# Decay rows of one half batch moved to a second set of matmuls, and its values loaded before its keys, in a fused attention and gated-FFN kernel

## The chip, the cores and the metric

The kernel runs on one core of one Trainium2 chip. The metric is device time in microseconds (us) of that core, lower is better. TensorE (PE) does the matmuls, its weight loads have a row of their own (PEld), VectorE (DVE) and ScalarE (ACT) do the elementwise work, GpSimd (POOL) and SyncE (SP) issue most of the DMAs. Each engine works through its own list of instructions in order; so does each DMA queue.

## What is computed

Eight batches, eight heads, 576 positions, head size 64. Attention has a causal mask and a decay that comes from forget gates `f`; its output is the input of a feed-forward block with a three-tap convolution as a gate:

```python
scores = q @ k.T / sqrt(64)
cum = cumsum(log(clip(f, 1e-4, 1.0)))
scores = where(causal, -1e9, scores + cum[..., :, None] - cum[..., None, :])
attn = softmax(scores);  x = (attn @ v)            # heads side by side: 8 x 576 x 512
h = relu(x @ w_in)                                 # 512 -> 1024
gate = sigmoid(conv3(h, conv_w))                   # along the sequence
out = (h * gate) @ w_out                           # 1024 -> 512
```

Inputs and output are FP32. The kernel works in BF16 and FP16 with FP32 sums.

## The kernel before

**Unit of loading: the half batch.** `hb` counts 16 half batches of four heads (`HH` = 4); `b = hb // 2` is the batch. `load_qk` (L106) brings q and k of a half batch by two transposing DMAs on SP's queue (L110), straight into matmul layout: 128 rows, of which the odd ones are the upper halves of the FP32 numbers (taken as BF16) and the even ones the lower halves. The tiles `stq`, `stk` form a ring of four (`RING`). `load_v` (L158) brings the values of a half or a whole batch by five DMAs on SP (L163) with 256-byte pieces; there are two such FP32 tiles, `vf`, one per batch in turn, and `cast_v` (L167) turns a half batch into FP16 `va` on DVE.

**The even rows carry the decay.** They hold lower halves that must go. `clamp` (L116) multiplies them by zero on DVE (L119), or a DMA from a zero tile `consts` does it (`fill`, L129, L132, issued by POOL): q is clamped for `hb` below `CLAMPS` = 8 and filled from there on, k is always clamped. The freed rows then take the decay: rows 96 and 98 of `stk` take the cumulated log gates as a high and a low BF16 part, row 126 of `stq` the high part of the query's, and the facing rows take the constants `PAIR` (about 1.002) and `MINUS`. So one matmul with 128 rows gives scores and decay together. `rows_of` (L135) issues these row loads on POOL, for `hb` = 1 from the SBUF tiles `khi_sb`, `klo_sb` (L140 to L142), later from a DRAM copy `kd` (L144, L146). For `hb` = 0 the rows come early, from a short cut (`rows_first`, L122).

**Work by head pair.** `i` = 0 to 31 counts pairs of heads. For each pair PE does the diagonal blocks of both heads (`diag_scores`, L326, mask added by L330), the blocks below the diagonal per head (`off_scores`, L315), once per half batch the last 64 positions (`tail_scores`, L301); all call `scores` (L296, matmul L298). The PSUM pool `sc` has two buffers. ACT takes the exponentials (L338, L324, L310), PE multiplies by the values (`pv`, L340, L356) into one PSUM buffer `O`, DVE divides by the row sums (`norm`, L359, L367 and L369) and so frees `O`.

**Feed-forward.** Per batch PE transposes the result (L393, L401), multiplies by `w_in` (`moe1`, L420, L425), ACT applies ReLU (L438), DVE does the convolution in two steps (L455, L457), ACT the tanh (L467), DVE the gate (L475), PE multiplies by `w_out` (`moe2`, L484, L487), ACT or DVE empties PSUM (`evac`, L503) and a DMA stores. These share two PSUM buffers `mm`; `ht` has four buffers.

**What sets the order.** The start (L188 to L269) is written out by hand. Everything after is a list of tasks with an engine cost, the tasks that must come first, a key (smaller goes first), buffers taken and given, and for loads a lag to landing. `play` (L713) runs through this list as in a small simulation, and the order in which it starts tasks is the order in which each engine gets its instructions. The numbers in it decide order alone; on the chip each instruction waits for what it needs. `CLAMPS`, `HALVES`, `LANDING`, `QUEUED` and `dma_free` are constants of this plan. In the order by hand, SP's queue holds: `f`, q and k of half batch 0 in two parts each, q and k of half batch 1 (`load_qk(1, 0, 4)`, L235), then the values of batch 0 in two halves (L251, L252). Ahead of these stands

```python
nc.vector.memset(vf_t[0][0:1, 0, 0, 0:1], 0.0)   # L250
```

a one-element write that makes the first load of values wait until DVE has come to that line. Similar one-element writes (`hold`, L149) make the loads of `w_in` and `w_out` wait (L631, L594).

Of the kernel before, what the change touches and what calls it, by code (L numbers as in the profile page):

```python
# [18 lines left out]
def kernel(  # L19
# [26 lines left out]
    HH = 4  # L46
# [88 lines left out]
    def rows_of(hb):  # L135

        tq, tk = stq_t[hb % RING], stk_t[hb % RING]
        c = slice(hb * HH, (hb + 1) * HH)
        if hb == 1:
            nc.gpsimd.dma_start(tk[96:97, 0:HS], khi_sb[c, :])  # L140
            nc.gpsimd.dma_start(tk[98:99, 0:HS], klo_sb[c, :])
            nc.gpsimd.dma_start(tq[126:127, 0:HS], khi_sb[c, :])  # L142
# [3 lines left out]
        nc.gpsimd.dma_start(bass.AP(tensor=tk.tensor, offset=int(tk.offset) + 96 * row, ap=[[2 * row, 2], [1, HS]]),  # L146
                            kd[:, c, :].rearrange("j h s -> j (h s)"))

    def hold(w):  # L149
# [391 lines left out]

    def fill_sources():
        z = consts.bitcast(FP32)
        nc.vector.memset(z, 0.0)
        nc.vector.memset(z[0:2, :], PAIR)
        nc.vector.memset(z[32:33, :], MINUS)
# [10 lines left out]

    last = None
    t_fsrc = task({"DVE": 3.1}, [], -9, fill_sources)
    for hb in range(NHB):  # L560
        key = 2 * hb - 5.5
        ring = [x for j in range(2) for x in t_qk[hb - RING, j]] if hb >= RING else []
        b = hb // 2
        even, landed = [], []
        for s in range(2):
            if hb == 1:
                x = task({"ACT": 0.01}, [], -9, lambda: None, lag=(0.3, 3.8)[s])
# [5 lines left out]
            if hb:  # L573
                t = (stq_t, stk_t)[s][hb % RING]
                rows = [(100, 14, 19)] if s else [(96, 15, 0)] + [(0, 48, 33)] * (hb >= CLAMPS)
                even.append(task({"POOL": 0.55 * len(rows)}, [t_fsrc, x], 2 * hb - 3.5,
                                 lambda t=t, rows=rows: [fill(t, *x) for x in rows],
                                 lag=LANDING + 1.0, dma=0.3 if s or hb < CLAMPS else 1.2))
            if hb and (s or hb < CLAMPS):
                even.append(task({"DVE": 0.9}, [x], (2 * hb - 3 if hb > 1 else -5) + 0.2 * s,  # L580
                                 lambda hb=hb, s=s: clamp(hb, s, 0, 4, 96)))
        t_half = None
        if b == 0 and hb < 2:
            t_half = task({"ACT": 0.01}, [], -9, lambda: None, lag=(6.5, 9.3)[hb])
# [11 lines left out]
        if hb:  # L596
            t_rows[hb] = even + [task({"POOL": 1.1 if hb > 1 else 1.6}, landed, 2 * hb - 3.6 if hb > 1 else -9 if hb > 1 else -1.0,
                                      lambda hb=hb: rows_of(hb), lag=LANDING + 1.0)]
        else:
            t_rows[hb] = []  # L600
        for p in range(2):
            t_cast[hb, p] = task({"DVE": 0.75 if p == 0 else 0.42},
                                 [t_half or t_v[b]] + ([t_pv[2 * hb - 5, 1]] if hb >= 3 else []), 2 * hb - 1.1 + 0.5 * p,
                                 lambda hb=hb, p=p: cast_v(hb, p, nc.vector), lag=0.2)

        for p in range(2):
# [9 lines left out]
            exps = {}  # L616
            x = task({"PE": 0.9}, t_rows[hb], i + 0.1, lambda i=i: diag_scores(i), take="sc")
            t_qk[hb, p] = [t_tail, x]
            mask = task({"ACT": 1.02}, [x], i + 0.1, lambda i=i: diag_exp(i), take="pm", give=[("sc", x)])
            for s in range(2):  # L620
                x = task({"PE": 0.46}, t_rows[hb], i + 0.2 + 0.4 * s, lambda i=i, s=s: off_scores(i, s),
                         take="sc")
                t_qk[hb, p].append(x)
                exps[s] = task({"ACT": 1.02}, [x] + ([t_pv[i - 2, s]] if i >= 2 else []), i + 0.2 + 0.4 * s,
                               lambda i=i, s=s: off_exp(i, s), give=[("sc", x)])
            for s in range(2):
# [3 lines left out]
                                  give=[("pm", mask)] if s else [])  # L630
            t_norm[i] = task({"DVE": 1.05}, [t_pv[i, 1]], i - 0.0, lambda i=i: norm(i) if i else [norm(i), hold(w_in_f16)],  # L631
                             take="xn" if i % PPB == 0 else None, give=[("O", t_pv[i, 0])])
            if i == 0:
                t_win = task({"POOL": 1.0}, [t_norm[0]], -0.5, lambda: nc.gpsimd.dma_start(
                    w_in_f16, moe_w_in.rearrange("(cc p) ff -> p cc ff", p=128)), lag=2.0, dma=6.5)
        if hb % 2:
            early, late = [t_norm[i - 3], t_norm[i - 2]], [t_norm[i - 1], t_norm[i]]
# [8 lines left out]

    start = [PPB * (b0 + nb) + 1.0 for b0, nb in GROUPS]
    start += [start[-1] + 4.0, start[-1] + 6.0]
    t_exp, t_late = [], []
    for g, (b0, nb) in enumerate(GROUPS):  # L650
# [39 lines left out]
        for c in chunks:  # L690
# [19 lines left out]

    AHEAD, QUEUED = 3.0, 8.0

    def play():  # L713
        busy = {"PE": 11.5, "ACT": 12.0, "DVE": 12.0, "POOL": 14.0, "SP": 19.0}
        ready = {e: [] for e in busy}
        dma_free, clock = 21.5, 0.0
        heap, order = [], []
# [111 lines left out]
```

## Time and profile before

| | |
|---|---|
| median of 6 runs | 272.46 us (271.78 to 274.11) |
| the profiled execution, own time | 272.23 us |
| its span, first to last instruction | 270.3 us |
| mean granted TensorE clock | 0.970 |
| busy: PE, DVE, ACT, POOL | 242.3, 227.0, 212.1, 60.5 us |
| DMA queue of SP: share of 16 engines' span | 67.7% |

Shares are of the span. The page cuts the span into 40 slices of 6.76 us and gives each engine's busy share in tenths; PEclk is the TensorE clock that was granted; the DMA row is the mean share of 16 DMA engines. A line of a timeline reads: start in us, duration in us, engine, line of the kernel, operation, what is written and read, how many; in brackets the engine's idle time just before and what ended it. Some matmul records are missing from a trace.

### The profile page before, as it was taken

How to read it: one execution, taken by the hardware profiler on the slowest of the kernel's cores; microseconds unless marked ns; L12 is line 12 of the kernel's file. 1: busy time of each engine (PE TensorE's matmuls, PEld its weight loads, DVE VectorE, ACT ScalarE, POOL GpSimd, SP SyncE). 2: the span in 40 equal slices, each digit the busy share in tenths (PEclk: the TensorE clock that was granted, in tenths of full speed). 3: DMA queues.
4: the chain of work that ended last, by engine and by line, in shares of the span. 5: the costliest groups of instructions: out<-in, count | busy, mean ns of one | idle time of the engine just before them, and what ended most of it. 6: DMA issues, size and time to landing. Idle time of an engine off the chain costs nothing.

```text
span 270.3 us, 6621 instructions
## 1 busy us (share of the span) xinstructions
PE 242.3 (90%) x2602; PEld 166.8 (62%) x2602; DVE 227.0 (84%) x401; ACT 212.1 (78%) x347; POOL 60.5 (22%) x124
## 2 busy tenths in 40 slices
PE   2677789776999999999999999999999999989990
PEld 1246557555777777676776677667776767654640
DVE  5864649979699999999989989999899999978751
ACT  5064649868879999989989899989989998577552
POOL 4391302451121240333315040405010100000000
PEclk9968979997999999999999999999999999999997
DMA  7999999999999999999999999999111201022015
GB/s 132 208 205 189 197 200 201 212 235 185 196 188 192 244 225 202 215 245 221 266 204 204 198 271 164 193 216 237 42 39 41 80 0 66 15 116 80 0 47 226
DMA packets 121284, 44.58 MB, mean 165 GB/s; under 512 B 115560, under 2 KB 116596, under 8 KB 121254
## 3 DMA queue, kind: packets, MB, share of 16 engines
q1 hardware_dynamic: 115088, 32.00, 67.7%
q0 software_dynamic: 5840, 12.01, 17.2%
q8 instruction: 20, 0.33, 0.5%
q10 hardware_dynamic: 326, 0.17, 0.3%
q14 instruction: 10, 0.08, 0.1%
HBM read 13.99 MB, written 9.58 MB: 87 GB/s over the span
## 4 chain that ended last, share of the span: by engine, by line
PE 67%; DMA 8%; issue 6%; DVE 6%; ACT 5%; SPq 5%; POOL 0%; ACTq 0%; DVEq 0%; POOLq 0%
PE mm L487 19%; PE mm L425 18%; PE sc L298 11%; PE O L356 9%; PE sc L330 4%; SPq L110 3%; DMA vf<-in_v_dram 3%; DMA stk<-in_k_dram 2%; PE sc L500 2%; DMA stq<-kd 2%; PE mm L393 2%; ACT po L324 1%; SPq L163 1%; DVE u L457 1%; ACT ht L438 1%
## 5 line engine op out<-in xcount | busy, mean ns | idle before, releaser
L425 PE MATMUL mm<-xt,w_in_f 128*128 128x288 f16 x512 | 79.5, 289 | 1.7 <-DVE xt L413 0.4
L298 PE MATMUL sc<-stq,stk 128*128 128x128 bf16 (+3 forms) x576 | 68.3, 245 | 7.3 <-ACT pm L338 4.7
L324 ACT ACTIVATE po<-sc 128x1024 f16<-128x1024 f32 x64 | 64.7, 1028 | 2.3 <-PE sc L298 1.8
L298 PEld LDWEIGHTS <-stk 128*128 128x128 bf16 x576 | 43.1, 100 | 29.6 <-issue 10.7
L438 ACT ACTIVATE ht<-mm 128x288 f16<-128x288 f32 x128 | 52.1, 414 | 11.4 <-PE mm L425 10.3
L487 PE MATMUL mm<-w_out_f,hg 128*128 128x512 f16 x248 | 58.4, 379 | 0.7 <-ACT xt L411 0.6
L425 PEld LDWEIGHTS <-w_in_f 128*128 128x128 f16 x512 | 47.7, 99 | 18.3 <-issue 3.3
L455 DVE SCALAR_TENSOR_TENSOR u<-ht,cwt 128x576 f32<-128x576 f16 x64 | 51.5, 811 | 5.4 <-ACT ht L438 4.7
L457 DVE SCALAR_TENSOR_TENSOR u<-ht,cwt,u 128x576 f32<-128x576 f16 x64 | 51.5, 811 | 0.5
L467 ACT ACTIVATE hg<-u,cwt 128x576 f16<-128x576 f32 x56 | 43.4, 779 | 2.3 <-DVE u L457 2.2
L475 DVE SCALAR_TENSOR_TENSOR hg<-hg,ht 128x576 f16<-128x576 f16 x56 | 41.7, 751 | 3.5 <-ACT hg L467 3.1
L338 ACT ACTIVATE pm<-sc 128x1024 f16<-128x1024 f32 x32 | 32.9, 1028 | 14.3 <-PE sc L298 14.2
L487 PEld LDWEIGHTS <-hg 128*128 128x128 f16 x248 | 23.6, 98 | 24.2 <-issue 0.9
L356 PE MATMUL O<-va,po 128*128 128x65 f16 x640 | 37.4, 196 | 1.1 <-ACT po L324 1.0
L356 PE MATMUL O<-va,pm 128*128 128x65 f16 x256 | 31.7, 196 | 2.9 <-DVE xn L369 1.7
L356 PEld LDWEIGHTS <-po 128*128 128x128 f16 x640 | 31.4, 99 | 2.1 <-ACT po L324 1.5
L132 POOL DMA_DIRECT2D stq<-consts x23 | 13.3, 583 | 75.0 <-DMA stq<-in_q_dram 28.9
L356 PEld LDWEIGHTS <-pm 128*128 128x128 f16 x256 | 24.6, 100 | 5.7 <-DVE xn L369 2.7
L369 DVE TENSOR_TENSOR xn<-O,rc 128x640 f16<-128x640 f32 x32 | 26.4, 824 | 1.1
L330 PE MATMUL sc<-trib,identb 128*128 128x512 bf16 x64 | 24.9, 390 | 2.0 <-ACT po L324 1.9
L511 ACT ACTIVATE ob<-mm 128x512 f32<-128x512 f32 x23 | 13.7, 598 | 11.0 <-PE mm L487 10.7
L522 POOL DMA_DIRECT2D out_dram<-ob x10 | 7.5, 749 | 41.5 <-ACT ht L438 19.7
(112 smaller groups left out, 223.2 us busy)
## 6 DMA issues: line engine op xcount, KB each, us to landing
vf<-in_v_dram SPq DMA_DIRECT2D x64, 128.0 KB, 4.0
out_dram<-ob POOLq DMA_DIRECT2D x10, 512.0 KB, 5.6
out_dram<-ob SPq DMA_DIRECT2D x10, 256.0 KB, 2.1
stq<-consts POOLq DMA_DIRECT2D x8, 216.0 KB, 4.6
vf<-in_v_dram SPq DMA_DIRECT2D x16, 64.0 KB, 5.3
w_in_f<-in_moe_w_in_dram POOLq DMA_DIRECT2D x1, 1024.0 KB, 10.7
w_out_f<-in_moe_w_out_dram POOLq DMA_DIRECT2D x4, 256.0 KB, 6.4
out_dram<-ob SPq DMA_DIRECT2D x2, 512.0 KB, 2.8
```

Source lines behind the costliest of these rows:

```text
L298: nc.tensor.matmul(sc, stk_t[hb % RING][:, k0:k0 + 128], stq_t[hb % RING][:, q0:q0 + w], start=start, stop=stop, skip_group_check=True)
L324: nc.scalar.activation(p_of[i, s][:, 0:1024], sc_of.pop((i, s)), AF.Exp, scale=SCALE)
L330: nc.tensor.matmul(sc[:, 512 * s:512 * (s + 1)], identb, trib, start=True, stop=False, skip_group_check=True)
L338: nc.scalar.activation(p_of[i, 2], sc_of.pop((i, 2)), AF.Exp, scale=SCALE)
L356: nc.tensor.matmul(O[:, s, 65 * Q:65 * (Q + 1)], w, va[:, h, m, :], start=(m == 0), stop=(m == Q))
L425: nc.tensor.matmul(ps[:, 0:w], w_in_f16[:, cc, 128 * ff:128 * (ff + 1)], xt[:, cc, w * t:w * (t + 1)], start=(cc == 0), stop=(cc == NCC - 1))
L438: nc.scalar.activation(ht[:, 0, HT_0 + w * t:HT_0 + w * (t + 1)], ps[:, 0:w], AF.Relu)
L455: nc.vector.scalar_tensor_tensor(u, hl, cwt[:, ff, 0:1], hc, op0=ALU.mult, op1=ALU.add)
L457: nc.vector.scalar_tensor_tensor(u, hr, cwt[:, ff, 1:2], u, op0=ALU.mult, op1=ALU.add)
L467: nc.scalar.activation(hv, u, AF.Tanh, scale=cwt[:, ff, 2:3])
L475: nc.vector.scalar_tensor_tensor(hv, hv, 1.0, hc, op0=ALU.add, op1=ALU.mult)
L487: nc.tensor.matmul(ps, chunk(g, ff, c), w_out_f16[:, ff, :], start=(ff == 0), stop=(ff == NFF - 1))
```

## The change

Half batch 1 no longer takes its decay in the even rows. Two new tiles, `dk` and `dq`, hold it: rows 0 and 1 of `dk` the high and low part of the keys' and row 2 a constant, rows 0 and 1 of `dq` a constant and row 2 the queries' high part; the rows of `dk` from 3 on are zero, those of `dq` meet these zeros. ACT writes the constants (three activations with scale 0), POOL loads the three rows. In `scores`, half batch 1 gets a second matmul of the same shape from these tiles, added in PSUM. Its q and k are clamped over all 128 rows; the two fills and the three row loads of before are gone.

The first half of batch 0's values is now loaded ahead of q and k of half batch 1, the second half after them, and the one-element write at L250 is gone. The zero tile `consts` is filled by three tasks after pair 1's `norm`, where one task did it at the start. Up to five pairs of extra matmuls without a use (`warm`) follow the last `pv` of half batch 0, with the key that goes last.

Numbers of the plan change too: `CLAMPS` 8 to 6 (q of half batches 6 and 7 filled by DMA, no longer clamped), `HALVES` 16 to 6 (from batch 3 on values are loaded by five DMAs of a whole batch, not ten of halves), keys of the clamps, casts, `norm`, ReLU, tanh, gate and `evac`, the starts of the feed-forward groups, `QUEUED` and `dma_free`, and the lags of the first loads.

```diff
+    dk_t = cpool.tile([128, HS + 64], BF16, name="dk")
+    dq_t = cpool.tile([128, HS], BF16, name="dq")
...
-        if hb == 1:
-            nc.gpsimd.dma_start(tk[96:97, 0:HS], khi_sb[c, :])
-            nc.gpsimd.dma_start(tk[98:99, 0:HS], klo_sb[c, :])
-            nc.gpsimd.dma_start(tq[126:127, 0:HS], khi_sb[c, :])
-            return
...
+    def decay_tiles(hb, dk, dq):
+        dec_of[hb] = dk, dq
+        for t, x in ((dk, 0.0), (dk[0:3], MINUS), (dq, PAIR)):
+            z = t.bitcast(FP32)
+            nc.scalar.activation(z, one1[0:z.shape[0]].broadcast_to(z.shape), AF.Copy, bias=x, scale=0.0)
+
+    def load_decay(hb):
+        (dk, dq), c = dec_of[hb], slice(HH * hb, HH * (hb + 1))
+        nc.gpsimd.dma_start(dk[0:1, 0:HS], khi_sb[c, :])
+        nc.gpsimd.dma_start(dk[1:2, 0:HS], klo_sb[c, :])
+        nc.gpsimd.dma_start(dq[2:3, 0:HS], khi_sb[c, :])
...
-    load_qk(1, 0, 4)
     for side in range(2):
         clamp(0, side, 0, 2)
     rows_first(0, nc.scalar)
+    load_v(0, 0, HH)
+    load_qk(1, 0, 4)
+    load_v(0, HH, H)
+    decay_tiles(1, dk_t, dq_t)
...
     rows_first(1, nc.gpsimd)
-    nc.vector.memset(vf_t[0][0:1, 0, 0, 0:1], 0.0)
-    load_v(0, 0, HH)
-    load_v(0, HH, H)
+    load_decay(1)
     nc.gpsimd.dma_start(kd[0], khi_sb)
...
+    def warm():
+        ps = mm_pool.tile([128, 512], FP32, name="mm")
+        for t in range(2):
+            nc.tensor.matmul(ps, identb, trib, start=True, stop=True)
...
         nc.tensor.matmul(sc, stk_t[hb % RING][:, k0:k0 + 128], stq_t[hb % RING][:, q0:q0 + w],
-                         start=start, stop=stop, skip_group_check=True)
+                         start=start, stop=stop and hb not in dec_of, skip_group_check=True)
+        if hb in dec_of:
+            dk, dq = dec_of[hb]
+            nc.tensor.matmul(sc, dk[:, k0:k0 + 128], dq[:, q0:q0 + w],
+                             start=False, stop=stop, skip_group_check=True)
...
-    CLAMPS, HALVES, LANDING = 8, 16, 3.0
+    CLAMPS, HALVES, LANDING = 6, 6, 3.0
+    WARM = {0: 5}
...
-    t_fsrc = task({"DVE": 3.1}, [], -9, fill_sources)
+        if hb == 2:
+            t_fsrc = None
+            for z in ((0, 96, 0.0), (0, 2, PAIR), (32, 33, MINUS)):
+                t_fsrc = task({"DVE": 1.03}, [t_norm[1], t_fsrc], 3.0, lambda z=z: fill_source(*z))
...
-                even.append(task({"DVE": 0.9}, [x], (2 * hb - 3 if hb > 1 else -5) + 0.2 * s,
-                                 lambda hb=hb, s=s: clamp(hb, s, 0, 4, 96)))
+                even.append(task({"DVE": 0.9}, [x], (2 * hb - 2 if hb > 1 else -5) + 0.2 * s,
+                                 lambda hb=hb, s=s: clamp(hb, s, 0, 4, 96 if hb > 1 else 128)))
...
-                                 [t_half or t_v[b]] + ([t_pv[2 * hb - 5, 1]] if hb >= 3 else []), 2 * hb - 1.1 + 0.5 * p,
+                                 [t_half or t_v[b]] + ([t_pv[2 * hb - 5, 1]] if hb >= 3 else []), 2 * hb - 0.6 + 0.5 * p,
...
-            t_norm[i] = task({"DVE": 1.05}, [t_pv[i, 1]], i - 0.0, lambda i=i: norm(i) if i else [norm(i), hold(w_in_f16)],
+            t_norm[i] = task({"DVE": 1.05}, [t_pv[i, 1]], i - 0.5, lambda i=i: norm(i) if i else [norm(i), hold(w_in_f16)],
...
+        if hb in WARM:
+            x = None
+            for _ in range(WARM[hb]):
+                x = task({"PE": 0.44}, [t_pv[2 * hb + 1, 1], x], 999, warm, take="mm", lag=0.05)
...
-    start = [PPB * (b0 + nb) + 1.0 for b0, nb in GROUPS]
-    start += [start[-1] + 4.0, start[-1] + 6.0]
+    start = [PPB * (b0 + nb) + x for (b0, nb), x in zip(GROUPS, (1.0, 1.0, 1.5, 1.5, 1.5, 1.0, 0.5, 0.5))]
+    start += [PPB * B + 5.0, PPB * B + 7.0]
...
-                relus.append(task({"ACT": 0.18 + w / 1200.0}, [x] + relus[0:1], key + 0.05 * t - 1.5,
+                relus.append(task({"ACT": 0.18 + w / 1200.0}, [x] + relus[0:1], key + 0.05 * t - 2.0,
...
-                     [x] + (t_tanh[0:1] or t_exp), key - 0.5, lambda g=g, ff=ff: tanh(g, ff),
+                     [x] + (t_tanh[0:1] or t_exp), key - 0.0, lambda g=g, ff=ff: tanh(g, ff),
...
-            t_gate[g, ff] = task({"DVE": 0.1 + n / 1800.0 if g == LAST else 0.2 + n / 1050.0}, [x], key - 1.5, lambda g=g, ff=ff: gate(g, ff),
+            t_gate[g, ff] = task({"DVE": 0.1 + n / 1800.0 if g == LAST else 0.2 + n / 1050.0}, [x], key - 0.0, lambda g=g, ff=ff: gate(g, ff),
...
-            x = task({"DVE": 0.62, "ACT": 0.57}, [x] + ([y] if c % 2 else []), key - 1.0,
+            x = task({"DVE": 0.62, "ACT": 0.57}, [x] + ([y] if c % 2 else []), key - 0.0,
...
-    AHEAD, QUEUED = 3.0, 8.0
+    AHEAD, QUEUED = 3.0, 10.0
```

More of the change, by code (lines that the diff above doesn't have):

```diff
@@ L147, in rows_of @@
                             kd[:, c, :].rearrange("j h s -> j (h s)"))
+    dec_of = {}
+    def decay_tiles(hb, dk, dq):
[8 more added lines that the diff above has]
+        nc.gpsimd.dma_start(dq[2:3, 0:HS], khi_sb[c, :])
     def hold(w):
@@ L540, in task, with fill_source @@
         return len(tasks) - 1
[L542 to L546, printed above, removed]
-    CLAMPS, HALVES, LANDING = 8, 16, 3.0
+    def fill_source(p0, p1, x):
+        nc.vector.memset(consts.bitcast(FP32)[p0:p1, :], x)
+    CLAMPS, HALVES, LANDING = 6, 6, 3.0
     HELD, POOLED = 4, 4
     WAITS = ((3, 0), (3, 1), (4, 0), (4, 1))
+    WARM = {0: 5}
     room = {"sc": 2, "O": 1, "mm": 2, "pm": 2, "xn": 2, "xt": 2, "u": 2, "ht": NHT,
@@ L558 @@
     last = None
-    t_fsrc = task({"DVE": 3.1}, [], -9, fill_sources)
+    t_dec = {1: task({"ACT": 0.01}, [], -99, lambda: None, lag=4.5)}
     for hb in range(NHB):
         key = 2 * hb - 5.5
+        if hb == 2:
+            t_fsrc = None
+            for z in ((0, 96, 0.0), (0, 2, PAIR), (32, 33, MINUS)):
+                t_fsrc = task({"DVE": 1.03}, [t_norm[1], t_fsrc], 3.0, lambda z=z: fill_source(*z))
         ring = [x for j in range(2) for x in t_qk[hb - RING, j]] if hb >= RING else []
@@ L566 @@
             if hb == 1:
-                x = task({"ACT": 0.01}, [], -9, lambda: None, lag=(0.3, 3.8)[s])
+                x = task({"ACT": 0.01}, [], -9, lambda: None, lag=(4.8, 7.6)[s])
             elif hb:
@@ L572 @@
                 landed.append(x)
-            if hb:
+            if hb > 1:
                 t = (stq_t, stk_t)[s][hb % RING]
@@ L579 @@
             if hb and (s or hb < CLAMPS):
-                even.append(task({"DVE": 0.9}, [x], (2 * hb - 3 if hb > 1 else -5) + 0.2 * s,
-                                 lambda hb=hb, s=s: clamp(hb, s, 0, 4, 96)))
+                even.append(task({"DVE": 0.9}, [x], (2 * hb - 2 if hb > 1 else -5) + 0.2 * s,
+                                 lambda hb=hb, s=s: clamp(hb, s, 0, 4, 96 if hb > 1 else 128)))
         t_half = None
         if b == 0 and hb < 2:
-            t_half = task({"ACT": 0.01}, [], -9, lambda: None, lag=(6.5, 9.3)[hb])
+            t_half = task({"ACT": 0.01}, [], -9, lambda: None, lag=(2.0, 11.0)[hb])
             t_v[b] = t_half
@@ L596 @@
         if hb:
-            t_rows[hb] = even + [task({"POOL": 1.1 if hb > 1 else 1.6}, landed, 2 * hb - 3.6 if hb > 1 else -9 if hb > 1 else -1.0,
-                                      lambda hb=hb: rows_of(hb), lag=LANDING + 1.0)]
+            t_rows[hb] = even + [task({"POOL": 1.1}, landed, 2 * hb - 3.6, lambda hb=hb: rows_of(hb), lag=LANDING + 1.0)
+                                 if hb > 1 else t_dec[hb]]
         else:
@@ L616 @@
             exps = {}
-            x = task({"PE": 0.9}, t_rows[hb], i + 0.1, lambda i=i: diag_scores(i), take="sc")
+            x = task({"PE": 1.33 if hb in t_dec else 0.9}, t_rows[hb], i + 0.1, lambda i=i: diag_scores(i), take="sc")
             t_qk[hb, p] = [t_tail, x]
@@ L620 @@
             for s in range(2):
-                x = task({"PE": 0.46}, t_rows[hb], i + 0.2 + 0.4 * s, lambda i=i, s=s: off_scores(i, s),
+                x = task({"PE": 0.89 if hb in t_dec else 0.46}, t_rows[hb], i + 0.2 + 0.4 * s, lambda i=i, s=s: off_scores(i, s),
                          take="sc")
@@ L635 @@
                     w_in_f16, moe_w_in.rearrange("(cc p) ff -> p cc ff", p=128)), lag=2.0, dma=6.5)
+        if hb in WARM:
+            x = None
+            for _ in range(WARM[hb]):
+                x = task({"PE": 0.44}, [t_pv[2 * hb + 1, 1], x], 999, warm, take="mm", lag=0.05)
+                gives = tasks[x][4]
+                gives.append(("mm", x))
         if hb % 2:
@@ L715, in play @@
         ready = {e: [] for e in busy}
-        dma_free, clock = 21.5, 0.0
+        dma_free, clock = 22.0, 0.0
         heap, order = [], []
```

## The prediction

> **What bounds the kernel now.** I read the 40 slices first, to see where engines are not full; then the busy times by stretch, cut where the granted clock changes; then the timeline of the stretch that is not full, for what each engine waits for there.
>
> ```profile
> PE   2677789776999999999999999999999999989990
> DVE  5864649979699999999989989999899999978751
> ACT  5064649868879999989989899989989998577552
> PEclk9968979997999999999999999999999999999997
> DMA  7999999999999999999999999999111201022015
> ```
>
> From slice 11 (about 67 us) to slice 38 PE stands at 9, with DVE and ACT close behind; before that no engine is full for long, while the DMA engines are full from the second slice to the 28th. So the time is: a start paced by data, then some 195 us in which PE, DVE and ACT are all nearly full. What is gained in the start shifts all the rest, as long as the next data are there.
>
> ```profile
> 11.50:15.00 3.50, 1.29 (x14) 0.93 (x15) 2.72 (x5) 1.11 (x2) 3.21 (x12) 0.99 1.17 235
> 15.00:18.40 3.40, 2.88 (x16) 1.41 (x16) 2.17 (x3) 2.12 (x3) 3.20 (x16) 0.50 1.00 173
> 18.40:21.80 3.40, 3.14 (x30) 2.23 (x29) 1.07 (x3) 2.63 (x3) 1.74 (x4) 0.50 1.04 210
> 21.80:35.40 13.60, 9.50 (x172) 7.48 (x169) 8.52 (x23) 6.54 (x8) 3.48 (x5) 1.00 1.24 201
> 35.40:38.80 3.40, 3.02 (x18) 1.98 (x17) 0.29 (x1) 1.84 (x3) 0.00 (x0) 0.51 1.30 133
> 38.80:62.70 23.90, 18.87 (x234) 13.95 (x232) 22.11 (x42) 20.06 (x34) 8.24 (x12) 1.00 1.21 216
> 66.20:260.00 193.80, 190.62 (x2056) 132.20 (x2053) 176.68 (x284) 168.63 (x285) 36.06 (x62) 1.00 0.78 154
> ```
>
> Columns: stretch, length, busy time of PE, PEld, DVE, ACT, POOL, granted clock, DMA share, GB/s. Between 21.8 and 35.4 us PE is busy 9.50 of 13.60 and DVE 8.52: this is half batch 1, and this is where the change works. Between 38.8 and 62.7 DVE is the full engine (22.11 of 23.90): it convolves batch 0 there, so an earlier end of half batch 1, which closes batch 0, starts the fullest engine earlier. After 66 us PE idles 3.2 us in all. The clock is halved in 15.0 to 21.8 and 35.4 to 38.8.
>
> ```profile
> 18.48 0.43 DVE L170 TENSOR_SCALAR va<-vf 128x512 f16<-128x512 f32 x1 [1.24 <-DMA vf<-in_v_dram]
> 19.64 0.50 POOL L142 DMA_DIRECT2D stq<-khi_sb  x1
> 23.55 0.20 PE L356 MATMUL O<-va,pm 128*128 128x65 f16 x1 [1.18 <-DVE w_in_f L151]
> 24.52 0.27 PE L304 MATMUL sc<-trit,identb 128*128 128x256 bf16 x1
> 30.86 0.87 DVE L119 TENSOR_SCALAR stq<-stq,lim 96x2304 uint16<-96x2304 uint16 x1
> 31.90 0.82 DVE L369 TENSOR_TENSOR xn<-O,rc 128x640 f16<-128x640 f32 x1
> 32.78 0.20 PE L356 MATMUL O<-va,pm 128*128 128x65 f16 x1 [1.36 <-DVE xn L369]
> 35.08 0.40 PE L393 MATMUL mm<-ident,xn 128*128 128x128 f16 x4 [0.95 <-DVE xn L369]
> 36.19 4.56 PE L425 MATMUL mm<-xt,w_in_f 128*128 128x288 f16 x24 [0.38 <-DVE xt L413]
> ```
>
> Half batch 1 begins at 24.52 us, for two reasons that end together: the last of its five small POOL loads is issued at 19.64 and, at the 3.7 us that the DMA view gives for it, lands at about 23.8; and PE, in order, first does the values of pair 1, which wait for `norm` of pair 0, which waited for the first values (cast at 18.48). Inside it PE waits 1.36 us because DVE clamps q of half batch 2 ahead of `norm`. Batch 0's feed-forward starts at 36.19.
>
> **Values ahead of keys.** Five loads of values now go out right behind the parts of half batch 0, at 7.5 to 10.3 us (0.55 each on SP, as at 13.13). A load took 3.6 us to land in that stretch: they are there near 14 instead of 18.5, so pair 0's values can be multiplied from about 17 us, not 20.71, and `norm` of pair 0 ends near 20, not 23.5. The keys pay: before, they landed at 16.34 and the values 2.1 us behind them, on engines that were full; so now the keys land 2.1 to 2.8 us later, 18.5 to 19.2. The removed L250 cost nothing: SP was not done with the keys until 13.0, DVE passed L250 at 11.07. SP's queue behind is as long as before, so half batch 2 (its key rows issued at 32.04, down about 6 us later) gains at most 1 us; I take 0.
>
> **Decay without rows.** Five POOL loads (two fills, three rows, 2.6 us of issue at 17.6 to 20.1) and their landing are gone from half batch 1; what is left ahead of its scores is the keys' clamp, 0.87 us (the 96-row clamp's time; I take it for 128 rows, since the columns are the same). Data are ready at about 20.1 instead of 23.8. PE can start when a score buffer comes free, at the half clock of that time near 21.9. Gain 2.6 us at this point, between 0 (if PE's work at half clock reaches further) and 3.7.
>
> **The second matmuls.** Per head four diagonal blocks (0.21 us from start to start, 28.09 to 28.30) and the off-diagonal ones (0.43 from start to start, 29.91 to 30.34), and 0.12 for the tail: 4 x 0.65 + 0.12 = 2.7 us of PE, 5.4 at half clock. ACT does not hide them: it needs 2.75 us per pair (three exponentials of 0.92), PE 2.7 before and 4.0 after. So they lie on the path. Half batch 1 took 24.52 to 35.04; less the idle (0.29, 0.32, 1.36, 0.95) PE worked 7.6. After: 7.6 + 2.7 + 1.0 (pair 1's values, which fall behind its start) = 11.3, plus 0.95 for the last `norm` and about 0.1 for other waits, since `norm` now goes ahead of the clamps. From 21.9 that is 34.2 us instead of 35.0: **0.8 us gained**. The bounds are a loss of 2.7 (no earlier start) and a gain of 3.
>
> **Moved and added around it.** ACT writes `dk` and `dq`: three activations of about 1184 columns, by the 128x1024 row 1.05 to 1.2 us each, 3.2 to 3.6 in all, from 9.0 (its last DMA issue) to 12.5; ACT stood idle until 13.89. Cost 0 with 1.3 us to spare; were it late, the first exponential would move by the excess. POOL issues the three decay rows (1.6 us) at about 12.7, when ACT is done; behind them wait the `kd` stores, the `va` memsets and the identities, 1.6 us later. The first `va` is needed at about 17 and is ready by 16, the identity at 26. Cost 0. The zero tile's 3 x 1.02 us leave DVE at 11.8 to 15.4, where it waited for data anyway, for the time after pair 1's `norm`, where it idles 0.91 and 2.13 us; POOL's fill for q of half batch 2 (27.17) and the rows behind may wait 1.5 us for it, but the key rows at 32.04 land last. Cost 0, at worst 1. The spare matmuls are ten of 0.22 us: 2.2 us if all stand in the way, at half clock 4.3; they go last in order, so 0.
>
> **The clock.** Here a rule of the Trainium skill is to be weighed. The page "TensorE: Matmul & The Clock Gate", section "Why this matters for your kernels", has it that drops of the clock are avoided as long as no idle gap exceeds about 3 us. By that no drop would follow 21.8 to 35.4, whose longest gaps are 1.36 and 0.95 us. The trace has the drop at 35.4, so this trace speaks against the rule, and the spare matmuls and the shorter gaps have something to win: from 36.19 the chain shows 16 matmuls of `moe1` in 3.42 us, 0.214 each, where 8 took 0.98 from start to start at full clock (42.12 to 43.10), 0.122 each: 1.5 us. By the rule the term is 0, by the row up to 1.5; I take **0.8 gained**.
>
> **Less clamping.** Two clamps of 0.87 us leave DVE (79.2 and 90.7 us). Fills of 216 KB take their place, 4.6 us to landing, hidden by a lead of 10 us or more: q of half batch 6 lay there at 79, its scores began at 91.5. In that stage PE and DVE are both full, so I count half: **0.9 gained** (0 to 1.7). Loading whole batches saves SP 25 issues of 0.52 us, but SP is paced by full DMA engines: 0. The odd half's keys come 3 us later on that queue, with a lead of 15 us at half batch 7 (85.5 to 100.6): 0.
>
> **The re-keyed plan.** `norm` and ReLU go earlier, clamps, casts, tanh, gate and `evac` later. One place is visible: POOL stood 3.68 us at 42.5 to 46.2 waiting for the hold on `w_out` behind DVE's work, and with it the rows of half batch 3, whose scores began at 54.5. A new order may take 3 us away or leave it: I count **0.6**. In the full stage at most the 3.2 us of idle PE can be won; a poor order can lose more. I take 0, from -3 to +5.
>
> Sum: 0.8 + 0.8 + 0.9 + 0.6 = 3.1 us from the profiled execution's 272.2 gives 269.1. The median lies 0.2 higher: **269.3 us**.
>
> **Rivals.** (1) *Loads rule the start.* Half batch 2's rows land near 38.5 and it starts at 40.6; DMA is full throughout. Then an earlier half batch 1 only lengthens a wait; only the clamps remain: 272.4 - 0.9 = 271.5. For it: the DMA row; against it: DVE is full from 38.8 with work that needs batch 0 and not half batch 2. (2) *Two PSUM buffers held longer, slower than before.* `evac` now gives way to other work of ACT and DVE, and the `mm` buffers are only two. There are 31 evacuations of 0.6 to 0.7 us on the path between `moe2` and the next matmul; each that lets a ReLU (0.41) or a tanh (0.78) pass returns its buffer so much later. From 0.1 us seen per evacuation it eats the 3.1 us; at 0.25 it costs 7.8 less the part that the other buffer covers, say 5: 269.3 + 5 = 274.3. Against it: the chain has little of `evac` in it now. (3) *Clock and hold both yield.* No half clock at 35 or at 63 (another 1.5), rows of half batch 3 three us earlier: 3.1 + 0.7 + 1.5 + 2.4 = 7.7 gained, 264.7.
>
> **How the numbers follow.** Forecast 0.52 (267.5 to 271.0), rival 1 0.14, rival 2 0.22, rival 3 0.12. A measurement of this kernel can tell about 0.5% (1.36 us) from no change: faster is the forecast and rival 3, 0.64; same is rival 1, 0.14; slower is rival 2, 0.22. Range 264.7 to 275.0: it takes in all but the ends of rivals 2 and 3.
>
> **What will show it.** Right if the first score of half batch 1 starts at 21 to 22.5 us, its keys land at 18.5 to 19.5 (clamp directly after), and batch 0's first `moe1` matmul starts at 34.5 to 35.5 with clock 1.0. Wrong if that matmul is not earlier than 36.2 (the second matmuls ate it all), if the first score of half batch 2 stays at 40.6 and that of half batch 5 at 77.7 (rival 1), or if PE idles more than 3.2 us between 66 us and 10 us before the end, with ACT or DVE `ob` as releaser (rival 2).

## The result, and the profile after

The changed kernel takes **275.13 us** in the median of 18 runs (273.35 to 290.35); the kernel before takes 272.93 us in 37 runs beside it. Its time is **1.0067 times** that of before (95% interval 1.0042 to 1.0091): slower, where 269.3 us had been forecast. The profile shown here is of a second set of runs of the same kernel (label `e1_after`, own time 274.75 us, span 272.4 us), because some executions of a kernel are longer than its fastest by 1.5% and more: the medians in this document count them and the ratios leave them out (15 of the 22 runs of `e9`, 11 of the 22 of `e11`), and the first profile of the changed kernel and those of `e4`, `e9` and `e11` are of such executions, so that only their first 50 us are read.

The 40 slices (each now 6.81 us), rows PE, clock and DMA:

```profile
PE   2658978599899999999999999999999999989991
...
PEclk9968999979999999999999999999999999999997
DMA  7999999999999999999999979995102202032016
```

PE is weaker than before in slices 3 and 8 (5 in each, 7 before), and the clock is halved for 6.8 us in slices 3 and 4, as long as before, and once more in slice 9. The busy times by stretch (columns as before the change: length, PE, PEld, DVE, ACT, POOL, clock, DMA share, GB/s):

```profile
11.50:15.00 3.50, 0.00 (x0) 0.00 (x0) 1.05 (x3) 2.23 (x2) 0.72 (x2) 1.00 1.24 200
15.00:18.40 3.40, 1.73 (x12) 1.25 (x13) 0.88 (x1) 1.45 (x3) 2.92 (x6) 0.68 1.28 222
18.40:21.80 3.40, 2.54 (x15) 1.16 (x14) 0.00 (x0) 2.98 (x4) 2.46 (x20) 0.50 1.21 241
...
66.20:260.00 193.80, 191.17 (x2100) 133.78 (x2097) 178.15 (x288) 169.28 (x290) 38.83 (x64) 1.00 0.79 155
```

In 11.5 to 15.0 us PE does nothing, where it worked 1.29 us before, and the next 3.4 us hold 1.73 instead of 2.88. From 66.2 on nothing is worse: PE idles 2.6 us there, 3.2 before. So the loss is at the very beginning. The first score before:

```profile
13.03 0.38 PE L298 MATMUL sc<-stq,stk 128*128 128x128 bf16 x4 [2.51 <-DMA stk<-klo]
```

and PE's timeline of the changed kernel, with the first score, the last wait in half batch 1 and the first `moe1`:

```profile
16.67 0.58 PE L318 MATMUL sc<-stq,stk 128*128 128x128 bf16 x4 [5.49 <-DMA stk<-klo]
...
37.74 0.20 PE L380 MATMUL O<-va,pm 128*128 128x65 f16 x1 [1.40 <-DVE xn L393]
41.47 5.50 PE L449 MATMUL mm<-xt,w_in_f 128*128 128x288 f16 x36 [0.38 <-DVE xt L437]
```

The first score of half batch 0, a step of which the prediction says nothing, starts at 16.67 us; before, it started at 13.03. It waits for the last of its decay rows (`stk<-klo`). Everything follows: `norm` of pair 0 starts at 24.63, where the forecast had it end near 20, and `moe1` at 41.47 instead of 36.19. The first values do come early, as forecast (DVE casts them at 12.39, before at 18.48), but there are no scores to multiply them with. Against the kernel before, the changed one is 3.6 us behind at the first score, 3.6 at half batch 4, 3.7 at half batch 15 and 2.3 at PE's last matmul.

ACT issues these rows. Its timeline before,

```profile
6.49 0.51 ACTq L125 DMA_DIRECT2D stq<-khi  x1
7.64 0.48 ACTq L126 DMA_DIRECT2D stk<-khi  x1
8.16 0.82 ACTq L127 DMA_DIRECT2D stk<-klo  x1
```

and after the change, where the rows are followed by `decay_tiles` (L154):

```profile
8.36 0.51 ACTq L127 DMA_DIRECT2D stq<-khi  x1
10.32 0.48 ACTq L128 DMA_DIRECT2D stk<-khi  x1
12.22 0.47 ACTq L129 DMA_DIRECT2D stk<-klo  x1
12.73 2.41 ACT L154 ACTIVATE dk<-one 128x1184 f32<-128x1184 f32 x2 [6.43 <-DMA vf<-in_v_dram]
15.05 1.14 ACT L154 ACTIVATE dq<-one 128x1152 f32<-128x1152 f32 x1
```

The three issues are 2 us apart instead of about 0.5, and the trace names a load of *values* as what released ACT. ACT neither reads nor writes values. The question is why it waits for them.

**Theory A, a shared set of completion semaphores.** A semaphore is a counter on which an engine can wait. The records of the trace name it for every DMA: in the built program those issued by SP or ACT signal their end on one of eight, 101 to 108, given out in turn; those of POOL have a set of their own, 111 to 118. Who takes a semaphore again waits until the DMA that had it last has landed. Before, the first two rows took semaphores 102 and 103 of loads that had landed at 5.27 and 3.75 us. In the changed kernel they take 106 of the second part of q (landed at 8.28 us), 108 of the first value load (10.24) and 103 of the fourth (12.20), and the records have ACT wait on just these three; it issues at 8.36, 10.32 and 12.22.

In the source the rows still stand ahead of the values. The turn does not follow the source: the five value loads have 108, 101, 102, 103 and 104, q of half batch 1 has 105, and only then comes 106, the first row. The built program has an order of its own. In the kernel before, with the one-element write at L250, all values but the first stood behind the rows in it: the rows had 102, 103 and 105, the first four value loads 104, 106, 107 and 108.

**Rivals.** B: the DMA engines are fuller, so the rows land later. D: ACT itself is in the way and delays the rows whatever the order; any other engine would issue them sooner. Or (C) the cause lies in the rest of the change: the second matmuls, the 128-row clamp and the hold on `w_out` in a new order, or the re-keyed plan in the full stage.

### The profile page after: what moved, and what is told of

It reads as the page before. It is cut to its first block, busy times and chain, and to the rows that moved or that the text cites. A ratio compares the mean times of both kernels' runs of the same rounds, so it can differ in the third digit from the quotient of the medians.

```text
span 278.2 us, 6653 instructions
## 1 busy us (share of the span) xinstructions
PE 248.1 (89%) x2648; PEld 170.2 (61%) x2648; DVE 224.5 (81%) x399; ACT 213.0 (77%) x349; POOL 58.5 (21%) x124
## 4 chain that ended last, share of the span: by engine, by line
PE 70%; DMA 10%; DVE 6%; ACT 6%; SPq 3%; issue 2%; POOL 0%; ACTq 0%
PE mm L449 18%; PE mm L511 18%; PE sc L318 13%; PE O L380 10%; PE sc L354 4%; DMA stk<-consts 4%; DMA stk<-in_k_dram 3%; SPq L112 2%; PE sc L524 2%; PE mm L417 2%; DMA stk<-klo 2%; DVE xn L393 1%; DVE u L479 1%; ACT pm L362 1%; DMA vf<-in_v_dram 1%
## 5 line engine op out<-in xcount | busy, mean ns | idle before, releaser
L318 PE MATMUL sc<-stq,stk 128*128 128x128 bf16 (+3 forms) x576 | 71.3, 249 | 12.0 <-DMA stk<-klo 4.8
L449 PE MATMUL mm<-xt,w_in_f 128*128 128x288 f16 x512 | 78.0, 286 | 3.0 <-ACT ht L462 1.1
L318 PEld LDWEIGHTS <-stk 128*128 128x128 bf16 x576 | 44.5, 101 | 33.3 <-issue 17.1
L462 ACT ACTIVATE ht<-mm 128x288 f16<-128x288 f32 x128 | 51.3, 413 | 8.2 <-PE mm L449 6.4
L362 ACT ACTIVATE pm<-sc 128x1024 f16<-128x1024 f32 x32 | 32.7, 1023 | 13.7 <-PE sc L318 11.5
L380 PEld LDWEIGHTS <-po 128*128 128x128 f16 x640 | 30.8, 98 | 1.7 <-ACT po L348 0.6
L354 PE MATMUL sc<-trib,identb 128*128 128x512 bf16 x64 | 25.5, 399 | 1.3 <-ACT po L348 1.2
L134 POOL DMA_DIRECT2D stq<-consts x24 | 12.4, 521 | 60.3 <-DMA stq<-in_q_dram 35.3
L535 ACT ACTIVATE ob<-mm 128x512 f32<-128x512 f32 x27 | 16.2, 599 | 9.5 <-PE mm L511 9.2
L391 DVE RECIPROCAL rc<-O 128x10 f32<-128x10 f32 x32 | 7.0, 218 | 16.0 <-PE O L380 15.7
```

Source lines behind the costliest of these rows:

```text
L354: nc.tensor.matmul(sc[:, 512 * s:512 * (s + 1)], identb, trib, start=True, stop=False, skip_group_check=True)
L362: nc.scalar.activation(p_of[i, 2], sc_of.pop((i, 2)), AF.Exp, scale=SCALE)
L380: nc.tensor.matmul(O[:, s, 65 * Q:65 * (Q + 1)], w, va[:, h, m, :], start=(m == 0), stop=(m == Q))
L449: nc.tensor.matmul(ps[:, 0:w], w_in_f16[:, cc, 128 * ff:128 * (ff + 1)], xt[:, cc, w * t:w * (t + 1)], start=(cc == 0), stop=(cc == NCC - 1))
L462: nc.scalar.activation(ht[:, 0, HT_0 + w * t:HT_0 + w * (t + 1)], ps[:, 0:w], AF.Relu)
```

## The experiments

All times are medians; the ratio is to the kernel before, run on the same chip in the same set.

| run | what it is | us | ratio (95%) |
|---|---|---|---|
| e1 | changed kernel again | 275.02 | 1.0093 (1.0063 to 1.0122) |
| e2 | changed, first rows issued by POOL | 268.29 | 0.9851 (0.9820 to 0.9882) |
| e3 | before, with the new load order alone | 274.38 | 1.0060 (1.0036 to 1.0084) |
| e4 | changed, with before's load order | 274.19 | 1.0053 (1.0030 to 1.0075) |
| e5 | before, first rows by POOL | 273.61 | 1.0046 (1.0021 to 1.0070) |
| e6 | e3, first rows by POOL | 275.48 | 1.0070 (1.0039 to 1.0101) |
| e7 | e4, first rows by POOL | 273.61 | 1.0058 (1.0036 to 1.0080) |
| e8 | e2 without the spare matmuls | 268.24 | 0.9889 (0.9850 to 0.9928) |
| e9 | changed, values later in the order | 273.16 | 0.9908 (0.9878 to 0.9937) |
| e10 | e2 with before's `CLAMPS` and `HALVES` | 272.79 | 1.0012 (0.9990 to 1.0035) |
| e11 | e2 without the second matmuls | 269.91 | 0.9882 (0.9860 to 0.9905) |
| e12 | e2 with before's keys of the feed-forward | 269.16 | 0.9896 (0.9864 to 0.9928) |

### e1: the changed kernel again

No edit. 

> The changed kernel itself, for an undisturbed profile. All theories: 0.4 to 0.9% slower than the kernel before. Theory A (the values' loads, put ahead, take the completion semaphores that half batch 0's decay-row loads on ACT wait for): the last of the three ACT row loads is issued near 12.2 us instead of 8.2, the first score starts near 16.7 instead of 13.0. Theory B (full DMA engines delay the landing of those rows): issue near 8.2, landing near 16. Theory C (the re-keyed plan loses in the full stage): first score near 13, PE idle over 3.2 us between 66 us and the end.

It took 275.02 us, 0.9% over the kernel before; its profile is the one above. The late issue and the first score at 16.67 us are what A expected; C's sign, more than 3.2 us of idle PE after 66 us, is absent.

### e2: the first rows from POOL

```diff
-    rows_first(0, nc.scalar)
+    rows_first(0, nc.gpsimd)
```

> The changed kernel with half batch 0's first row loads issued by POOL, whose loads have semaphores of their own. Theory A: the rows land near 12.5 to 13, the first score starts at 12.5 to 13.3, and the 3.6 us come back: 1.3% below the changed kernel, near 271.5 us, 0.995 of before. Theory B: the rows land near 16 all the same, time as the changed kernel, 1.007. Theory C: the start is earlier, the total stays above 1.003.

**268.29 us**, 1.5% faster than before and 6.7 us faster than the changed kernel, by three loads of 2.2 KB each. The gain is nearly twice what was expected. POOL has its own semaphores and waits for nothing but the data, as theory A has it. POOL's timeline of e2:

```profile
6.79 0.70 POOL L127 DMA_DIRECT2D stq<-khi  x1 [2.80 <-DVE stq L121]
7.59 0.54 POOL L128 DMA_DIRECT2D stk<-khi  x1
8.12 0.52 POOL L129 DMA_DIRECT2D stk<-klo  x1
```

And PE's, its first score and its first `moe1`:

```profile
11.92 0.38 PE L318 MATMUL sc<-stq,stk 128*128 128x128 bf16 x4 [0.17 <-DMA stk<-klo]
...
34.99 5.50 PE L449 MATMUL mm<-xt,w_in_f 128*128 128x288 f16 x36 [0.38 <-DVE xt L437]
```

The first score is 4.75 us earlier than in e1, `moe1` of batch 0 6.5 us, and PE's last matmul 6.6 us (259.7 against 266.3): the delay is carried to the end undiminished. The clock is 0.996 in the mean (e1: 0.975), with no half clock until 263 us. Theory B is at most a small part: the DMA share from 11.5 to 15.0 us is 1.24 in both, and the last row lands 3.7 us after its issue here and 4.4 in e1. Of the 4.75 us the issue makes 4.1 (8.12 against 12.22).

### e3: the new load order in the kernel before

```diff
-    load_qk(1, 0, 4)
     for side in range(2):
         clamp(0, side, 0, 2)
     rows_first(0, nc.scalar)
+    load_v(0, 0, HH)
+    load_qk(1, 0, 4)
+    load_v(0, HH, H)
...
-    nc.vector.memset(vf_t[0][0:1, 0, 0, 0:1], 0.0)
-    load_v(0, 0, HH)
-    load_v(0, HH, H)
```

> The kernel before with nothing changed but the order of the loads: first half of the values ahead of half batch 1's keys, the one-element write gone. Theory A: first score near 16.7, some 3 us slower than before, ratio 1.008 to 1.015. Theory B: the same time, but the ACT row loads are issued as early as before. Theory C: ratio 0.995 to 1.003.

ACT's timeline of e3:

```profile
8.36 0.57 ACTq L125 DMA_DIRECT2D stq<-khi  x1
10.35 0.47 ACTq L126 DMA_DIRECT2D stk<-khi  x1
12.20 0.47 ACTq L127 DMA_DIRECT2D stk<-klo  x1
```

The load order alone moves ACT's issues, and the first score to 16.50. So this edit by itself makes the rows late. But the kernel loses only 1.6 us by it (0.6%), about half of what was expected: half batch 2 starts 2.4 us later than before (43.0 against 40.6), half batch 4 only 0.5 (65.5 against 65.0). In the plan of before most of the delay is taken up again by half batch 4, in this trace; it is of an execution of 272.49 us, 1.9 below the median, and does not show where the others lose.

### e4: the rest of the change, with before's load order

```diff
+    load_qk(1, 0, 4)
     for side in range(2):
         clamp(0, side, 0, 2)
     rows_first(0, nc.scalar)
-    load_v(0, 0, HH)
-    load_qk(1, 0, 4)
-    load_v(0, HH, H)
...
+    nc.vector.memset(vf_t[0][0:1, 0, 0, 0:1], 0.0)
+    load_v(0, 0, HH)
+    load_v(0, HH, H)
...
-                x = task({"ACT": 0.01}, [], -9, lambda: None, lag=(4.8, 7.6)[s])
+                x = task({"ACT": 0.01}, [], -9, lambda: None, lag=(0.3, 3.8)[s])
...
-            t_half = task({"ACT": 0.01}, [], -9, lambda: None, lag=(2.0, 11.0)[hb])
+            t_half = task({"ACT": 0.01}, [], -9, lambda: None, lag=(6.5, 9.3)[hb])
```

> The changed kernel with the load order of before (keys of half batch 1 first, values held by the one-element write, and the plan's lags of before for these four loads); second matmuls, new keys and all else stay. Theory A and B: first score near 13.0, ratio 0.985 to 0.998, for all else was to gain 1 to 4 us. Theory C: ratio 1.003 or more.

274.19 us, against the expectation: the rest does not gain anything without the early values, although the rows are not late here (ACT issues them at 6.53, 7.61 and 8.12 us). Its DVE timeline shows one wait that is new:

```profile
22.28 0.43 DVE L183 TENSOR_SCALAR va<-vf 128x512 f16<-128x512 f32 x1 [2.25 <-DMA vf<-in_v_dram]
...
24.12 0.20 DVE L392 RECIPROCAL rc<-O 128x10 f32<-128x10 f32 x1
```

The cast of the second half's values stands ahead of `norm` of pair 0 in DVE's order and waits for its load; `norm` comes at 24.12, before at 22.42, and half batch 2 at 45.2, before at 40.6. It is not the whole reason: in e7, which has the same order, `norm` comes at 22.27 and half batch 2 still at 44.2. The rest stays open.

### e5, e6, e7: rows from POOL in the kernels that lack one half

The one-line edit of e2, in the kernel before (e5), in e3 (e6) and in e4 (e7).

> The kernel before with half batch 0's first row loads issued by POOL, nothing else. In the kernel before these loads waited for no load of values, so theory A gives little: first score within 1 us of 13.0, ratio 0.99 to 1.003. If the engine that issues them is what counts (rival D: ACT's own queue is slow, the semaphores are not the point), the first score comes near 12 and the ratio near 0.985, as in the changed kernel with these loads on POOL.

> The kernel before with the new load order and the first row loads on POOL. Theory A: the start comes back from 16.5 to 12 to 13 us; the order of loads by itself then costs or gains under 1 us: ratio 0.992 to 1.003, at least 0.5% under the new order with the rows on ACT (1.006). Theory B or D: 1.004 or more, or as low as 0.987.

> The changed kernel with the load order of before and the first row loads on POOL. If the rest of the change loses only because its plan expects the values early (theory A with an interaction): still 1.000 to 1.006, since half batch 1's values come at 22 to 24 us and DVE casts them ahead of the first norm. If the rest gains by itself: 0.99 or less.

None gains: 273.61, 275.48 and 273.61 us. Taken with e1 to e4 and before, these are all eight combinations of three edits (load order, rest, POOL). Seven lie at 1.000 to 1.009; only all three together lie at 0.985. For e6 that misses the expectation (0.992 to 1.003) and lies where theories B or D were to put it; yet its rows are not late (first score at 11.85 us). The traces of e5 and e6 show what takes the early start away. The first score of half batch 1 in e5, and in e6:

```profile
24.93 0.28 PE L298 MATMUL sc<-stq,stk 128*128 128x64 bf16 x4 [2.43 <-DMA stq<-khi_sb]
...
27.43 0.37 PE L297 MATMUL sc<-stq,stk 128*128 128x64 bf16 x4 [3.76 <-DMA stq<-khi_sb]
```

PE has finished half batch 0 and waits for the last of the five POOL loads of half batch 1, so that this score is no earlier than before (24.62). These are the loads that the second tiles do away with; in e2 the same score starts at 20.36. So, by these traces, the early rows help only where the second tiles are there too. In e6, where the keys of half batch 1 also come later, three stretches at half clock (3.4 us from 16.2, 6.8 from 26.5, 3.4 from 40.1) are added, with half batch 2 at 45.3. In e7 half batch 1 is early (19.47), but the values of half batch 0 are not: DVE casts them at 18.03, in e2 at 12.81.

### e8: without the spare matmuls

```diff
-    WARM = {0: 5}
+    WARM = {}
```

> The changed kernel with the first row loads on POOL and without the spare matmuls (WARM empty); everything else stays. If the spare matmuls are what keeps the clock at 1.0 from 13 to 66 us: a half clock near 30 to 36 us comes back and the time rises by 1 to 2 us (ratio to before 0.989 to 0.993). If the earlier start and the shorter gaps do it: clock stays at 1.0, time within 0.5 us of the version with them (0.985).

268.24 us against 268.29 for e2. A half clock appears at 62.9 us for 3.4 us, and the median does not show it. By the ratios (0.9889 and 0.9851, each uncertain by 0.3 to 0.4%) the spare matmuls may bring about 1 us or nothing.

### e9: rows from ACT, values later in the order

```diff
-    load_v(0, 0, HH)
-    load_qk(1, 0, 4)
-    load_v(0, HH, H)
...
+    nc.vector.memset(vf_t[0][0:1, 0, 0, 0:1], 0.0)
+    load_v(0, 0, HH)
+    load_qk(1, 0, 4)
+    load_v(0, HH, H)
     nc.vector.tensor_tensor_scan(cum, one1[0:BH]
```

The one-element write holds the loads back until DVE is at its scan, so that they come later in the order; the rows stay on ACT.

> The changed kernel, first row loads on ACT as it has them, but with the one-element write back, placed after DVE's cumulated sum, so that the values' loads come later in the order of semaphores and in time (near 9.4 us). The last row load then waits for a part of q of half batch 0 instead of for a load of values. Theory A: it is issued near 8.5 to 9 instead of 12.2, the first score starts near 13, and most of the loss comes back although ACT still issues the rows: ratio 0.987 to 0.998. Theory D (ACT's queue itself is slow with these loads): first score stays near 16.5, ratio 1.006 to 1.01.

ACT's timeline of e9:

```profile
6.51 0.52 ACTq L127 DMA_DIRECT2D stq<-khi  x1
7.13 0.54 ACTq L128 DMA_DIRECT2D stk<-khi  x1
7.96 0.47 ACTq L129 DMA_DIRECT2D stk<-klo  x1
```

ACT issues as early as before, and the first score starts at 10.71 us: theory D falls, ACT is quite able to issue these rows in time. The third row waits for the semaphore of the second part of q (landed at 7.94), not for a value. So it is the place in the order that makes the rows late, not the engine. The time of the kernel settles less. The runs reach from 267.96 to 282.03 us without a clear step between; their median, 273.16, lies 1.9 us below e1 and 1.0 above the kernel before, and the ratio of 0.9908 rests on the seven fastest. That this version keeps what e2 gains is not shown.

### e10: before's clamps and halves

```diff
-    CLAMPS, HALVES, LANDING = 6, 6, 3.0
+    CLAMPS, HALVES, LANDING = 8, 16, 3.0
```

> The changed kernel with the first row loads on POOL and CLAMPS, HALVES at 8 and 16 as before. If two clamps less on DVE are worth what the prediction says: 0.5 to 1.7 us slower than with 6 and 6 (268.3), ratio 0.987 to 0.991. If the full stage does not feel them: within 0.5 us.

272.79 us, where 0.5 to 1.7 us of loss were expected: without these two constants e2 loses 4.5 us, all of its gain. By stretches, the line of e2 for 80 to 160 us,

```profile
80.00:160.00 80.00, 80.00 (x922) 56.94 (x920) 75.38 (x125) 71.56 (x123) 23.35 (x40) 1.00 1.20 228
```

and that of e10:

```profile
80.00:160.00 80.00, 77.71 (x900) 55.14 (x899) 72.80 (x122) 70.94 (x119) 24.41 (x41) 1.00 1.19 221
```

PE is busy throughout in e2, and idles 2.3 us in e10. e10 reaches half batch 5 as early as e2 (74.9 and 75.2 us; before 77.7), is 2.7 us behind it at half batch 8 (114.6 against 111.8) and 4.9 at half batch 15 (216.3 against 211.4). So in these traces the constants do not make the lead, they keep it. Both constants were put back at once; which one counts was not tried.

### e11: without the second matmuls

```diff
-                         start=start, stop=stop and hb not in dec_of, skip_group_check=True)
-        if hb in dec_of:
-            dk, dq = dec_of[hb]
-            nc.tensor.matmul(sc, dk[:, k0:k0 + 128], dq[:, q0:q0 + w],
-                             start=False, stop=stop, skip_group_check=True)
+                         start=start, stop=stop, skip_group_check=True)
```

This leaves the decay out of the scores of half batch 1.

> The changed kernel with the first row loads on POOL and without the second matmuls, so the decay is left out of half batch 1's scores; order and all else stay. If the second matmuls lie on the path at 2.7 us, half batch 1 ends 2 to 2.7 us earlier; the total falls by as much only if nothing else holds half batch 2 (ratio 0.976 to 0.980). If loads hold half batch 2 (it starts near 41 in this kernel as in the one before): total within 1 us of 268.3.

269.91 us, no faster than with them, though the runs scatter (266.51 to 274.21). Its trace has a half clock of 6.8 us from 29.3 and half batch 2 at 42.3 (e2: 41.3). So taking these matmuls away gives no time back here; whether it is the emptier PE that loses the clock, or chance, one trace cannot tell.

### e12: before's keys of the feed-forward

The keys of ReLU, tanh, gate and `evac` and the starts of the groups as before:

```diff
-            x = task({"DVE": 0.62, "ACT": 0.57}, [x] + ([y] if c % 2 else []), key - 0.0,
+            x = task({"DVE": 0.62, "ACT": 0.57}, [x] + ([y] if c % 2 else []), key - 1.0,
```

and likewise ReLU -2.0 to -1.5, tanh -0.0 to -0.5, gate -0.0 to -1.5, all group starts +1.0.

> The changed kernel with the first row loads on POOL and the keys of before for ReLU, tanh, gate and evac and the starts of before for the feed-forward groups. If the new keys lose in the full stage (the slower rival of the prediction): faster than 268.3, by up to 3 us. If they gain there: slower by 1 to 4 us, with more idle PE after 66 us.

269.16 us against 268.29; the intervals of the ratios overlap. The new keys do no harm that shows; by the medians they bring 0.9 us, by these runs perhaps nothing.

## Why the prediction was wrong, point by point

**The step that failed: "Values ahead of keys".** "The removed L250 cost nothing: SP was not done with the keys until 13.0, DVE passed L250 at 11.07" looks at SP's queue and at DVE, but the edit puts five loads, in the order of the built program, ahead of another queue's loads as well: the three rows that ACT issues. They have no queue in common with the values; they share the eight completion semaphores. The missing term is 3.6 us at the first score (13.03 to 16.67), 4.75 against e2. Against e2 it then grows: `norm` of pair 0 comes at 24.63 in e1 and at 18.15 in e2, 6.5 us, while half batch 0 works for 6.8 us at half clock in e1 (from 16.3) and at full clock in e2. The time of the kernel shows 275.02 - 268.29 = 6.7 us. e2, e3 and e9 show the cause of the late first score from three sides: without the shared semaphores the delay is gone, with nothing but the load order it is there, and with the values later in the order it is gone again. That it costs the whole kernel 6.7 us is measured by e2 alone, in the changed plan; in the plan of before it costs 1.6 (e3).

**"ACT writes `dk` and `dq` ... from 9.0".** It wrote them from 12.73 to 16.2, behind the late rows, and POOL's decay rows, which wait for them, went out at 15.43 instead of 12.7. The cost of 0 with "1.3 us to spare" hung on the same unseen wait. In e2 ACT is done at 9.8.

**Keys at 18.5 to 19.2 us, clamp directly after.** In e2 the clamp stands at 19.16. In e1 it stands at 25.63. DVE's timeline of e1 shows why:

```profile
16.82 0.88 DVE L121 TENSOR_SCALAR stq<-stq,lim 128x2304 uint16<-128x2304 uint16 x1 [3.24 <-DMA stq<-in_q_dram]
24.63 0.22 DVE L391 RECIPROCAL rc<-O 128x10 f32<-128x10 f32 x1 [6.93 <-PE O L380]
...
25.63 0.88 DVE L121 TENSOR_SCALAR stk<-stk,lim 128x2304 uint16<-128x2304 uint16 x1
```

DVE waits 6.93 us for PE to finish pair 0, with `norm` ahead of the clamp of the keys in its order. So half batch 1, which the forecast has wait for its keys alone, waits for half batch 0.

**Why the delay is not taken up again.** In the plan of before the clamp of half batch 2's keys stands ahead of batch 0's convolution (32.64 us), in the changed plan behind its first step (44.16 in e1, 37.69 in e2), and the zero tile is filled behind pair 1's `norm`. So half batch 2 follows batch 0's feed-forward by order: e1 is behind e2 by 6.5 us at half batch 1, 6.5 at 2, 5.8 at 4 and 6.8 at 15. In e3 it is made good by half batch 4. That the order of DVE does it is read from the two traces; it was not tried alone.

**The rest of the sum: near in the total, and in part by luck.** With the rows on POOL the time is the forecast one: 268.29 us for 269.3 (own range 267.5 to 271.0), `moe1` at 34.99 (34.5 to 35.5) at full clock, half batch 1 at 20.3 (21 to 22.5 forecast). "Decay without rows" had the mechanism right: e5 and e6 show the wait that it takes away. But the lead does not arise as it was summed. Half batch 2 starts at 41.3 us in e2, 0.7 later than before; the lead comes behind it, 1.6 us at half batch 3, 2.6 at 5 and 3.1 at 15. The 0.9 us for the clamps and values was far too little: e10 gives 4.5. The 2.7 us for the second matmuls on the path are not confirmed: without them nothing is gained (e11). The 0.6 us for `w_out` is not there as a shorter wait: POOL waits 5.01 us for the first hold in e2 and 3.68 before, though it ends 0.95 us earlier; in e1 it waits 10.19 us and ends 5.5 us later. And the lead of 15 us for the keys of half batch 7 was about 13: before, these keys land at 87.5 us and are read at 100.6; nothing hangs on it here.

**The clock.** e2 has no half clock before 263 us and e8, without the spare matmuls, none before 62.9, so by that trace the spare matmuls are not what keeps the clock up in the start. What does stays open. Between 21.8 and 35.4 us PE is busy 9.50 of 13.60 us in the kernel before, with a longest gap of 1.36, and the clock is halved at 35.4. In e2 the figures are 11.73 and 1.40, and no drop follows; in e5 they are 8.24 and 2.43, and no drop follows before 63.9. So neither the longest gap nor the share of busy time tells these three apart. What the clock contributes to e2's gain was not separated.

**The rivals.** The time fell on the side of rival 2, by none of its mechanism: e12 shows no cost of the later `evac`, and PE idles less after 66 us than before. Rival 1 is half right of e2: half batch 2 is no earlier (41.3 us), half batch 5 is (75.2 against 77.7). What holds the plan of before back in e5 is not its wait for the rows of half batch 2, but for those of half batch 1. Rival 3's clock came in e2; its earlier rows of half batch 3 did only in part: that half batch starts at 53.0 in e2, 54.5 before.

## What to carry to other kernels

When a DMA is moved in the order, or a write that held it back is taken out, list which DMAs of every engine that shares its completion semaphores now come behind it, and what each of them has to wait for: here three 2.2 KB loads whose own lines nobody had touched cost 6.7 us of 275. The order that counts is that of the built program, not of the source. In the profile such a wait shows as an engine released by a transfer whose data it does not use. And an improvement that depends on a plan must be tried with the plan: of eight combinations of three edits only the complete one was faster, and each single edit was slower.

## What the runs showed of the hardware

- In this built program a DMA that takes a completion semaphore still in use waits in its issuing engine: ACT's issues went from 6.49, 7.64 and 8.16 us to 8.36, 10.32 and 12.22, each within 0.1 us after the landing of the load that held the semaphore, and everything behind it on ACT waited as well.
- Loads of 2.2 KB landed 3.5 to 4.4 us after their issue from ACT and 4.1 to 5.0 from POOL in e1 between 5 and 20 us, with the DMA engines full. The three rows themselves took 3.5 to 4.4 us from ACT in e1 and 3.2 to 3.7 from POOL in e2, where they go out up to 4.1 us earlier.
- ACT wrote a constant of 1184 FP32 columns in 1.2 us (2.41 for two, over 128 and over 3 rows), the larger end of the estimate.
